# Another order for a fused decay-attention and mixture-of-attention kernel

## The chip, the cores and the metric

The kernel runs on one core of a Trainium2 chip. The metric is the device time of one execution in microseconds (us). Three executions of the kernel before took 305.31, 306.22 and 306.68 us; their median is 306.22 us.

## The reference

Inputs are r, k and v of shape (4 batches, 8 heads, 768 positions, 48 values), a decay w and a bonus u for each head and value, and the weights of four attention experts. The first part is a linear attention with decay; the second takes its output as x (768 rows of 384 for each batch).

```python
for t in range(S):
    kt, vt, rt = (k[:, :, t], v[:, :, t], r[:, :, t])
    cur = np.einsum('bhd,bhe->bhde', u[None] * kt, vt)
    y[:, :, t] = np.einsum('bhd,bhde->bhe', rt, state + cur)
    state = w[None, :, :, None] * state + np.einsum('bhd,bhe->bhde', kt, vt)
...
logits = x @ w_gate            # top 2 of 4 experts, softmax over the two
for e in range(E):
    q, k, v = x @ wq[e], x @ wk[e], x @ wv[e]
    scores = scale * (q @ k.transpose(0, 2, 1))     # causal
    a = softmax(scores)
    out += gate[e] * (a @ v @ wo[e])
```

## The kernel before, in words

The 768 positions of a batch are cut into six chunks of 128, 24 in all; three chunks make a group, of which there are eight. Work is written as small steps, each a Python generator; a step is named with its arguments, as a_quarters,1 (chunk 1) or m_scores,7,1,2 (group 7, expert pair 1, chunk 2 of the group).

The first part, for chunk n: load_chunk loads k and r by DMA from SP's queue (L285, L287), load_vh the values (L292), load_vs a second copy with the halves swapped, for the first six chunks by two copies on ACT (L306). a_decay multiplies k and r by tables of powers of w (DVE for early chunks, else POOL). a_transpose turns k and r on PE (L513) and ACT copies them into kt, rt and rx (L519, L532, L536). a_quarters multiplies them on PE, first k with r (L552), then k with the values (L560). DVE masks the first (a_mask) and sums the second into the running state z (a_sum). a_out multiplies both with values and state (L585, L589), a_add adds the bonus term on DVE, and a_xt turns the result on PE (L620) and copies it on ACT. a_ku and a_own make the bonus term on POOL and DVE.

The second part, for group G: m_values (L686) and m_proj (L661) make values, queries and keys on PE; each product is three matmuls of rounded and rest parts. m_gate ranks the experts on DVE. m_scores makes scores on PE (L738), masks them on DVE (L743) and takes their exponential on ACT (L748). m_weigh scales them on POOL (L761). m_turn turns them on PE (L770), with a copy on ACT (L773). m_av multiplies them with the values (L791) and splits the result into yh (ACT, L798) and yl (DVE, L800). m_out is the last product (L814 to L816), copied on ACT and written by a DMA on SP.

warm_up (six bf16 matmuls of 512 columns, L319) and keep (four transposes, L360) are PE work whose result nobody uses.

What sets the order is the string ORDER: each word is one piece of a step, up to the step's next yield, and the pieces are written in this order, so each engine executes its own in this order. The hex digits behind a slash are the numbers of the buffers or PSUM banks that the piece takes from the rotating ones (the pools have fixed sizes, as eight banks). There is no planner and no scheduler behind it: a wait on an engine holds all that stands behind it there.

## Time and profile before

| | |
|---|---|
| Median of three runs | 306.22 us |
| Span of the profiled execution | 304.7 us |
| PE busy | 292.3 us, 96% |
| DVE, ACT, POOL busy | 206.0, 213.6, 173.2 us |
| DMA moved | 24.83 MB, mean 81 GB/s |

The span is the time from the first to the last instruction of one profiled execution; the page gives no other time for that execution, and the median of the runs stands 1.5 us above it. Busy times of the engines overlap; an engine's idle time matters only where it delays the one that the others wait for. [...] A row of the timeline gives start, duration, engine, line, operation, operands, count, and in brackets the idle time before it and what ended it.

### The profile page before, as it was taken

The numbers are of one execution on the slowest core, as the hardware profiler recorded it, in microseconds if no ns is written. First come the engines' busy times: TensorE is split into PE (matmuls) and PEld (weight loads), VectorE is DVE, ScalarE is ACT, GpSimd is POOL, SyncE is SP. The second block draws the span as 40 slices with busy tenths as digits, with TensorE's granted clock in tenths as the row PEclk, the third lists the DMA queues.
The fourth block names the chain that finished last, engine by engine and source line by source line (L and its number), as shares of the span: only waits on it lengthen the run. The fifth ranks groups of instructions, "written<-read, shape, count | busy, mean of one in ns | idle before, by whom it ended". The sixth has DMA issues, their size and how long they took to land.

```text
span 304.7 us, 13045 instructions
## 1 busy us (share of the span) xinstructions
PE 292.3 (96%) x5518; PEld 248.8 (82%) x5518; DVE 206.0 (68%) x676; ACT 213.6 (70%) x509; POOL 173.2 (57%) x227
## 2 busy tenths in 40 slices
PE   6879999999999999999999999999999999999996
PEld 3669989887898787888789787899799777997775
DVE  7867888889946478477686559468867277675510
ACT  2844687897596694946758794768869775669961
POOL 2969547872995923874454694956292624216420
PEclk9965999999999999999999999999999999999999
DMA  8986324661527327405440436564101200001012
GB/s 157 219 188 118 80 55 107 120 122 25 108 56 166 72 41 159 105 17 105 93 106 1 80 69 141 111 123 102 41 3 41 54 2 31 0 25 56 23 60 77
DMA packets 103310, 24.83 MB, mean 81 GB/s; under 512 B 99794, under 2 KB 103252, under 8 KB 103252
## 3 DMA queue, kind: packets, MB, share of 16 engines
q1 hardware_dynamic: 102688, 23.90, 36.6%
q8 instruction: 43, 0.70, 1.0%
q10 hardware_dynamic: 564, 0.10, 0.2%
q14 instruction: 15, 0.12, 0.1%
HBM read 19.28 MB, written 4.72 MB: 79 GB/s over the span
## 4 chain that ended last, share of the span: by engine, by line
PE 80%; DVE 6%; ACT 5%; issue 2%; POOL 1%; ACTq 0%; DVEq 0%; POOLq 0%
PE banks L661 16%; PE banks L791 11%; PE banks L738 10%; PE banks L686 9%; PE banks L770 8%; PE banks L589 4%; PE banks L552 4%; PE banks L585 4%; PE banks L814 4%; PE banks L513 3%; PE banks L816 3%; PE banks L815 3%; PE banks L560 2%; PE banks L620 2%; ACT rx L536 1%
## 5 line engine op out<-in xcount | busy, mean ns | idle before, releaser
L761 POOL TENSOR_SCALAR pr<-pr,f,gate 128x128 f32<-128x128 f32 (+5 forms) x96 | 67.7, 719 | 72.2 <-DVE f L755 48.7
L743 DVE CUSTOM_DVE_ANT_0 pr<-banks,after 128x256 f32<-128x256 f32 (+5 forms) x96 | 56.5, 620 | 26.7 <-PE banks L738 18.8
L748 ACT ACTIVATE pr<-pr,nm 128x512 f32<-128x512 f32 (+5 forms) x96 | 63.4, 663 | 8.1 <-DVE nm L743 7.7
L773 ACT ACTIVATE pt<-banks 128x768 f32<-128x768 f32 (+1 forms) x64 | 45.6, 731 | 14.8 <-PE banks L770 14.1
L738 PE MATMUL banks<-tk,tq 64*128 64x384 f32 (+3 forms) x384 | 41.5, 338 | 0.2
L791 PE MATMUL banks<-pt,vv 128*64 128x384 f32 (+2 forms) x324 | 40.7, 393 | 0.7 <-DVE yl L800 0.7
L791 PEld LDWEIGHTS banks<-pt,vv 128*64 128x64 f32 x324 | 20.6, 136 | 16.6 <-issue 12.3
L661 PE MATMUL banks<-xt_hi,wqk_hi 128*128 128x384 f32 x96 | 33.5, 349 | 0.6 <-DVE nm L743 0.6
L738 PEld LDWEIGHTS banks<-tk,tq 64*128 64x128 f32 x384 | 30.7, 186 | 3.5 <-issue 1.4
L770 PE MATMUL banks<-ident,pr 64*128 64x64 f32 x672 | 31.6, 227 | 0.9 <-DVE xt_lo L631 0.5
L661 PE MATMUL banks<-xt_hi,wqk_lo 128*128 128x384 f32 x96 | 32.3, 337 | 0.0
L661 PE MATMUL banks<-xt_lo,wqk_hi 128*128 128x384 f32 x96 | 32.3, 336 | 0.0
L770 PEld LDWEIGHTS banks<-ident,pr 64*128 64x128 f32 x672 | 26.2, 139 | 7.1 <-issue 4.2
L612 POOL TENSOR_TENSOR z<-z,w 128x192 f32<-128x192 f32 x20 | 10.1, 506 | 30.4 <-DVE z L608 19.4
L483 POOL TENSOR_TENSOR ku<-kdbuf,uw 128x384 f32<-128x384 f32 x24 | 25.0, 1045 | 2.6 <-DVE banks L492 1.9
L476 POOL TENSOR_TENSOR rdbuf<-rdbuf,tab_r 128x384 f32<-128x384 f32 x22 | 22.7, 1038 | 5.7 <-DMA rdbuf<-in_r_dram 5.7
L585 PE MATMUL banks<-vhbuf,sm 64*64 64x48 f32 x384 | 25.7, 226 | 0.1
L485 POOL TENSOR_TENSOR ku<-ku,rdbuf 128x384 f32<-128x384 f32 x24 | 24.9, 1039 | 1.3
L585 PE MATMUL banks<-vsbuf,sm 64*64 64x48 f32 x384 | 25.2, 226 | 0.0
L686 PE MATMUL banks<-wv_hi,xt_hi 128*128 128x260 f32 x72 | 22.4, 312 | 0.1
L585 PEld LDWEIGHTS banks<-vhbuf,sm 64*64 64x64 f32 x384 | 21.5, 141 | 0.3 <-issue 0.3
L476 POOL TENSOR_TENSOR kdbuf<-kdbuf,tab_k 128x384 f32<-128x384 f32 x21 | 21.5, 1027 | 0.0
(125 smaller groups left out, 723.9 us busy)
## 6 DMA issues: line engine op xcount, KB each, us to landing
kdbuf<-in_k_dram SPq DMA_DIRECT2D x24, 192.0 KB, 3.3
rdbuf<-in_r_dram SPq DMA_DIRECT2D x24, 192.0 KB, 3.6
vhbuf<-in_v_dram SPq DMA_DIRECT2D x24, 192.0 KB, 3.7
out_dram<-o SPq DMA_DIRECT2D x23, 192.0 KB, 1.9
vsbuf<-in_v_dram SPq DMA_DIRECT2D x36, 96.0 KB, 3.2
pr<-in_moe_wv_dram SPq DMA_DIRECT2D x1, 384.0 KB, 4.7
pr<-in_moe_wq_dram SPq DMA_DIRECT2D x1, 384.0 KB, 5.3
pr<-in_moe_wk_dram SPq DMA_DIRECT2D x1, 384.0 KB, 5.4
```

Of the source, the lines that this page charges most:

```text
L476: nc.gpsimd.tensor_tensor(t[:, :, :D], t[:, :, :D], (tab_k, tab_r)[which], op=OP.mult)
L483: nc.gpsimd.tensor_tensor(ku, kd[:, :, :D], uw, op=OP.mult)
L585: nc.tensor.matmul(o, st["sm", n][par][rows, p // 2, i], values, start=fresh, stop=True)
L661: nc.tensor.matmul(ps, a[:, t, m0:m0 + P], x[:, t, :], start=i == 0, stop=i == n - 1)
L686: nc.tensor.matmul(ps, x[:, t, cols], a[:, t, :], start=m == 0, stop=m == n - 1)
L738: nc.tensor.matmul(ps[par][:, n0:n1], tq[rows, part, q], tk[rows, key, n0:n1], start=i == 0, stop=i == 2)
L743: nc.vector.tensor_tensor_reduce(pr_[:, :N], ps[par], after[:, S - N:], 1.0, 3e38, op0=OP.add, op1=OP.min, accum_out=nm)
L748: nc.scalar.activation(pr_[:, :N], pr_[:, :N], AF.Exp, bias=nm, scale=-1.0, accum_out=sums[:, e, j, 0:1])
L761: nc.gpsimd.tensor_scalar(p[:, :N], p[:, :N], f[:, i], gate[:, i, e:e + 1], op0=OP.mult, op1=OP.mult)
L770: nc.tensor.transpose(both[:, x, half], mg[G]["p", e, j][rows, i * C:(i + 1) * C], ident[rows, rows])
L773: nc.scalar.activation(pt.rearrange("s (x half c) -> s x half c", x=n, half=2), both, AF.Copy)
L791: nc.tensor.matmul(psy[par * HD:par * HD + HD, j0 * C:j1 * C], vv[:, i % GC, e, :], mg[G]["t", e, i][:, (j0 - max(0, i - g * GC)) * C:(j1 ...
```

## The change

The string ORDER is replaced: the pieces of all steps stand in another order, and most of them take other buffers and banks of the same pools. The sizes of the pools, the steps and the instructions within a step stay. The table has three lines more, so a line number of the new kernel is three higher than the same line's number before. Its first lines, before and after:

```diff
-warm_up/2 make_ones make_ident load_chunk,0 load_w/0 load_w make_before clear pad,4 pad,0 load_uw powers table,0/0
-powers load_chunk,0 keep,2/2 warm_up/7 warm_up warm_up warm_up load_vh,0 warm_up warm_up table,0 table,1/1 table,1
+make_ident load_w/0 load_chunk,0 warm_up/6 make_ones clear pad,4 warm_up/7 warm_up pad,0 load_w a_transpose,0/4
+load_chunk,0 load_v/7 make_lower powers load_uw table,0/2 table,0 table,1/0 table,1 a_transpose,0/0 a_transpose,0/3
+a_transpose,0/0 make_before table,0/0 load_chunk,1 a_decay,0,0 hi_v load_chunk,1 load_vh,0 powers load_vh,2 table,1
...
```

On PE at the start, from the first a_quarters on, the order before is a_quarters,0 (L552, L560), a_transpose,1 (L513) and a_out,0 (L589 and on). In the rows kdbuf_135 to kdbuf_138 and rdbuf_139 to rdbuf_142 hold k and r, vhbuf_143 to vhbuf_146 the values, of chunks 0 to 3 in turn:

```order
L552 MATMUL banks<-rt_91,kt_89 64x64 x16
L560 MATMUL banks<-vhbuf_143,kdbuf_135 48x48 x16
L513 MATMUL banks<-ident,kdbuf_136 128x64 x8
L513 MATMUL banks<-ident,rdbuf_140 128x64 x8
L589 MATMUL banks<-z_102,rt_91 64x48 x2
L585 MATMUL banks<-vhbuf_143,sm_97 64x48
```

After, from behind a_transpose,1 on (L319 has become L322, the warm-up; L552 L555, L560 L563, L513 L516, L589 L592):

```order
L322 LDWEIGHTS pr_70
L322 MATMUL banks<-pr_70 128x512
L322 LDWEIGHTS pr_70
L322 MATMUL banks<-pr_70 128x512
L555 MATMUL banks<-rt_92,kt_89 64x64 x16
L563 MATMUL banks<-vhbuf_144,kdbuf_136 48x48 x16
L516 MATMUL banks<-ident,kdbuf_137 128x64 x8
L516 MATMUL banks<-ident,rdbuf_141 128x64 x8
L592 MATMUL banks<-z_103,rt_91 64x48 x2
L588 MATMUL banks<-vhbuf_143,sm_97 64x48
```

Four of the six warm-up matmuls have moved behind a_transpose,1, and a_quarters,1 and a_transpose,2 now stand ahead of a_out,0.

On SP's queue of loads at the start, before, from the third DMA to the weights of the values (pr6):

```order
L292 DMA vhbuf0_143<-in_v_dram 128x8x48
L285 DMA kdbuf1_136<-in_k_dram 128x8x48
L287 DMA rdbuf1_140<-in_r_dram 128x8x48
L285 DMA kdbuf2_137<-in_k_dram 128x8x48
L287 DMA rdbuf2_141<-in_r_dram 128x8x48
L292 DMA vhbuf1_144<-in_v_dram 128x8x48
L292 DMA vhbuf2_145<-in_v_dram 128x8x48
L285 DMA kdbuf3_138<-in_k_dram 128x8x48
L287 DMA rdbuf3_142<-in_r_dram 128x8x48
L443 DMA pr6_70<-in_moe_wv_dram 128x12x64
```

After, from the third DMA to the values of chunk 1 (vhbuf1):

```order
L446 DMA pr7_71<-in_moe_wv_dram 128x12x64
L447 DMA wg_166<-in_moe_w_gate_dram 128x3x4
L288 DMA kdbuf1_136<-in_k_dram 128x8x48
L290 DMA rdbuf1_140<-in_r_dram 128x8x48
L295 DMA vhbuf0_143<-in_v_dram 128x8x48
L295 DMA vhbuf2_145<-in_v_dram 128x8x48
L288 DMA kdbuf3_138<-in_k_dram 128x8x48
L290 DMA rdbuf3_142<-in_r_dram 128x8x48
L288 DMA kdbuf2_137<-in_k_dram 128x8x48
L290 DMA rdbuf2_141<-in_r_dram 128x8x48
L295 DMA vhbuf1_144<-in_v_dram 128x8x48
```

The weights have moved from twelfth to third place, and the values of chunk 1 from eighth to thirteenth, behind those of chunk 2 and behind k and r of chunks 3 and 2.

On PE near the end, before, from the last transposes (m_turn,7,3,2, L770) over m_out,6,2 (L814 to L816) to the first matmuls of the last m_av (L791):

```order
L770 MATMUL banks<-ident,pr_70 128x64 x2
L770 MATMUL banks<-ident,pr_66 128x64 x4
L814 MATMUL banks<-wo_hi,yh_82 128x384
L815 MATMUL banks<-wo_lo,yh_82 128x384
L816 MATMUL banks<-wo_hi,yl_83 128x384
L814 MATMUL banks<-wo_hi,yh_81 128x384
L815 MATMUL banks<-wo_lo,yh_81 128x384
L816 MATMUL banks<-wo_hi,yl_84 128x384
L791 MATMUL banks<-pt_75,vv_109 64x128
L791 MATMUL banks<-pt_79,vv_109 64x128
L791 MATMUL banks<-pt_75,vv_109 64x128
L791 MATMUL banks<-pt_79,vv_109 64x128
```

After, from the first part of the last m_av (L794, was L791) to the two m_turn steps behind it (L773, was L770):

```order
L794 MATMUL banks<-pt_79,vv_109 64x128
L794 MATMUL banks<-pt_75,vv_109 64x128
L794 MATMUL banks<-pt_79,vv_109 64x128
L794 MATMUL banks<-pt_75,vv_109 64x128
L794 MATMUL banks<-pt_78,vv_109 64x128
L794 MATMUL banks<-pt_76,vv_109 64x128
L794 MATMUL banks<-pt_78,vv_110 64x128
L794 MATMUL banks<-pt_76,vv_110 64x128
L773 MATMUL banks<-ident,pr_70 128x64 x2
L773 MATMUL banks<-ident,pr_68 128x64 x4
L773 MATMUL banks<-ident,pr_67 128x64 x2
L773 MATMUL banks<-ident,pr_64 128x64 x4
```

The m_out has left this place, the first part of the last m_av has moved ahead of two m_turn steps, and these now stand between its first and its second part.

## Rows read from the trace of the kernel before

**Rows 1.** The page: span, busy share of engines, granted clock, instruction queue.

```profile
span 304.7 us, 13045 instructions
...
PE 292.3 (96%) x5518; PEld 248.8 (82%) x5518; DVE 206.0 (68%) x676; ACT 213.6 (70%) x509; POOL 173.2 (57%) x227
...
PEclk9965999999999999999999999999999999999999
...
q8 instruction: 43, 0.70, 1.0%
```

**Rows 2.** Stretches: length, busy us of PE, PEld, DVE, ACT, POOL, clock, DMA share, GB/s.

```profile
7.00:16.00 9.00, 6.72 (x208) 5.46 (x206) 6.81 (x16) 7.39 (x19) 8.20 (x13) 1.00 1.07 212
...
17.00:18.00 1.00, 1.00 (x52) 1.00 (x52) 0.92 (x3) 0.96 (x3) 0.14 (x1) 0.50 1.18 258
...
22.00:26.00 4.00, 3.51 (x87) 3.23 (x88) 2.78 (x5) 2.05 (x5) 3.92 (x5) 0.50 0.86 166
...
50.00:150.00 100.00, 98.59 (x2051) 84.74 (x2049) 72.36 (x242) 73.38 (x177) 64.50 (x82) 1.00 0.46 96
150.00:290.00 140.00, 139.43 (x2359) 117.29 (x2357) 91.96 (x314) 104.33 (x248) 75.11 (x95) 1.00 0.25 58
```

**Rows 3.** Timeline of PE, first 31 us: start us, duration us, line, count, idle before.

```profile
3.90 2.77 PE L319 MATMUL banks<-pr 128*128 128x512 bf16 x6
...
9.71 0.69 PE L552 MATMUL banks<-rt,kt 48*64 48x64 f32 x32
...
10.70 0.46 PE L513 MATMUL banks<-ident,kdbuf 64*128 64x64 f32 x8
...
11.79 0.26 PE L589 MATMUL banks<-z,rt 48*64 48x48 f32 x2 [0.38 <-ACT z L604]
...
12.86 0.46 PE L513 MATMUL banks<-ident,kdbuf 64*128 64x64 f32 x8
...
14.10 0.36 PE L560 MATMUL banks<-vhbuf,kdbuf 64*48 64x48 f32 x16
16.18 0.40 PE L560 MATMUL banks<-vhbuf,kdbuf 64*48 64x48 f32 x16 [1.72 <-issue]
...
22.36 0.58 PE L620 MATMUL banks<-ident,ownv 64*128 64x64 f32 x6 [0.74 <-DVE ownv L596]
22.73 0.64 PE L513 MATMUL banks<-ident,kdbuf 64*128 64x64 f32 x8
...
23.73 0.46 PE L589 MATMUL banks<-z,rt 48*64 48x48 f32 x8
...
25.82 0.58 PE L686 MATMUL banks<-wv_hi,xt_hi 128*128 128x260 f32 x1
...
28.06 1.13 PE L552 MATMUL banks<-rt,kt 48*64 48x64 f32 x32
...
29.77 0.58 PE L620 MATMUL banks<-ident,ownv 64*128 64x64 f32 x6
...
30.95 0.39 PE L686 MATMUL banks<-wv_hi,xt_hi 128*128 128x260 f32 x1
```

**Rows 4.** SP's own timeline: the issue of vhbuf1 and its neighbour.

```profile
6.34 1.77 SPq L292 DMA_DIRECT2D vhbuf<-in_v_dram  x2
```

**Rows 5.** The page on such loads: count, KB each, median us to landing.

```profile
vhbuf<-in_v_dram SPq DMA_DIRECT2D x24, 192.0 KB, 3.7
```

**Rows 6.** Groups by form: count, busy us and mean ns, idle before.

```profile
L773 ACT ACTIVATE pt<-banks 128x768 f32<-128x768 f32 x48 | 38.4, 811 | 9.6 <-PE banks L770 9.0 <-PE banks L791 0.5
...
L798 ACT ACTIVATE yh<-banks 128x384 fp32r<-128x384 f32 x15 | 7.3, 485 | 5.9 <-PE banks L791 5.9
...
L306 ACT ACTIVATE vsbuf<-vhbuf 64x192 f32<-64x192 f32 x12 | 4.4, 363 | 0.2
```

**Rows 7.** Timeline of PE near the end: first and second part of the last m_av.

```profile
293.45 1.09 PE L791 MATMUL banks<-pt,vv 128*64 128x128 f32 x16
295.25 1.31 PE L791 MATMUL banks<-pt,vv 128*64 128x128 f32 x20 [0.70 <-DVE yl L800]
```

## The prediction

> **What bounds the kernel now.** I read the page first: the span is 304.7 us and PE (TensorE) is busy for 292.3 of it, 96%; DVE, ACT and POOL stay at 57 to 70% [rows 1]. So the matrix engine is the bound, and a new order can only matter where PE waits or where its clock is low. The clock row is all nines but for the third and fourth digit, 15.2 to 30.5 us [rows 1]. [...] What is to be won is therefore in the first 31 us; behind it lie 2.0 us of visible idle time in 240 (1.41 + 0.57).

> In the timeline of PE one sees what went before the drop. [...] At full clock come a_quarters,0 (9.71 to 10.70), a_transpose,1, a_out,0 (11.79 to 12.86). Then, in the middle of a_quarters,1, between two matmuls of the same line, PE stands still for 1.72 us until 16.18 "<-issue": it waited for nothing that another engine did [rows 3]. PE's instructions come by DMA queue q8: 43 packets for 5518 matmuls and 5518 weight loads, 257 instructions each [rows 1]; and the DMA engines are full in this stretch (share 1.07) [rows 2]. I read the wait as a late packet of instructions. In the stretch from 17 us the clock is at half; PE then waits again (0.74 us before 22.36), is without a listed wait from 25.82, and by the digits the clock is back at about 30.5 us.

> The price of the half clock comes from equal steps at both levels [rows 3]: a_out 1.07 us at full (chunk 0, which has 48 of the usual 64 matmuls) and 2.09 at half (chunk 2, 23.73 to 25.82); a_transpose 0.71 (10.70 to 11.79 less its 0.38 wait) and 1.00 (22.73 to 23.73); a_quarters 0.99 and 1.71 (28.06 to 29.77); m_values 2.24 at half (25.82 to 28.06), so some 1.2 at full; a_xt 0.37 at half (22.36 to 22.73) and 0.2 at full.

> **The change, part by part.** No instruction is added on PE but their order is new throughout; the tables of numbers choose other buffers and banks. I split the sum in the start, the middle and the tail.

> *The start, to the point where before stands at 30.95 us.* Four things move. keep (four transposes) leaves the start and goes to the middle, where it costs some 0.2 us of PE. Of the six warm-up matmuls four now stand behind a_transpose,1. On SP the weights wv (384 KB) and chunks 2 and 3 stand ahead of vhbuf1, the values of chunk 1. And a_quarters,1 and a_transpose,2 stand ahead of a_out,0 on PE.

> vhbuf1 was issued at 6.34 with its neighbour [rows 4], and such a load takes 3.7 us to land [rows 5]: about 10 us. It was the eighth tile and is now the thirteenth, wv counted as two. A tile of 192 KB (196,608 bytes) at 212 GB/s [rows 2] takes 0.93 us, so five tiles cost 4.6 us: about 14.6 us. a_quarters,1 needs it on PE, and the ACT copy into vsbuf1 (load_vs) too; ACT works its queue in order, and behind that copy stand tab_k and the copy that a_out,0 wants. Four copies at 0.36 [rows 6] and tab_k at much the same make 16.3 us for the start of a_out,0, where before it started at 11.79. The matmuls of a_quarters,1 and a_transpose,2 are done by then. So a wait for data stands where the wait for instructions stood. The new order has issued as many PE instructions as before had at that wait only inside a_out,0, at about 17 us, which is later than the packet came before (16.18). I take the packet's wait as gone, with 0 to 1.7 us as its bounds.

> [...]

> From 16.3 us I add up in the new order, at half clock: a_out,0 1.6 (48 of 64 of 2.09), a_transpose,3 1.0, a_xt,0 0.4, a_quarters,2 1.7, a_out,1 2.1: 23.1 us. No step of these waits for the step just ahead of it: chunk 3's transposes stand between a_out,0 and a_xt,0, and a_quarters,3 between a_out,1 and a_out,2, so the 0.74 us that a_xt,1 waited has cover. Before, the clock came back some 5 us after PE's last wait (25.82); a run of work without a wait begins at 16.3 to 17.6 us here. I therefore take the clock as back at about 22.4. Then a_out,1 ends 22.8, and at full clock come a_quarters,3 1.0, a_out,2 1.1 (the 1.07 row), a_xt,1 0.2, m_values,0,0 1.2, a_out,3 1.1, a_transpose,4 0.7: 28.1 us. Before has the same done at 30.95 but for a_out,3 (1.1 still owed) and with a_xt,2 (0.2) done in addition: the new order is ahead by 30.95 - 28.1 + 1.1 - 0.2 = 3.7, less keep 0.2: **-3.5 us**. The bounds: at half clock until 30.7 the same sum ends at about 31.7, which makes 0; at full clock from 16.3 on it ends at about 26.0 and makes -5.7; each us of half clock beyond 30.7 costs another 0.5.

> *The middle.* The PE work is the same and DVE, ACT and POOL have room; what can change are short waits. The nearest to one that I find are three: m_av,3,1,0,3 now follows m_turn,3,3,1 directly, whose bank ACT must copy first (0.81 [rows 6]; two thirds of the m_av's own matmuls come ahead of it): 0.2. m_out,2,1 stands one step behind m_av,2,1,0,3, whose copy takes 0.49 on ACT [rows 6] before DVE can subtract: 0.3. a_quarters,5 stands close behind a_transpose,5: 0.2. Of before's 2.0 us idle [rows 2] some will go and others come; I take these as even. Sum **+0.7**, bounds -2.0 (all idle gone) and +3 (as much again as there is, and the three at full price).

> *The tail.* Before, PE waits 0.70 us for DVE's yl ahead of the second part of m_av,7,1 [rows 7]. Two m_turn steps now stand there and cover it. They were taken from the place ahead of the first part, which now follows m_turn,7,3,1 at once, with ACT copies of 0.81 to wait for: 0.6, two copies less the matmuls that lie beside them. **-0.1**, bounds -0.7 and +0.9.

> The sum: 304.7 - 3.5 + 0.7 - 0.1 = 301.8 us of span. The median of the runs is 306.22, 1.5 above the span of the profiled execution; I keep that 1.5 and predict **303.3 us**.

> **The rivals.** *The start stays as it is.* For it: PE waits for data between 13 and 16.3 us in the new order, as it waited for instructions before, and in the stretch from 22 to 26 us before it was busy for 3.51 of 4 and the clock did not come [rows 2]; small matmuls may not bring it back, and m_values comes at about the same time in both. Against it: the waits behind 17.6 us have cover. It makes 304.7 + 0.7 - 0.1 + 1.5 = 306.8.

> *Slower: the clock comes late.* With only two warm-ups at the start PE stands idle from the first transposes until DVE's tables are ready, so the early steps run at half clock too, and the wait for vhbuf1 breaks the work again; if the clock is back only at 34 us or later, 3.4 us at half cost 1.7, and a late packet at the new place up to 1.7 more: 306.8 + 1.7 + 0.3 to 1.7, some 309. It decides from the point where the clock is still at half beyond 31 us. For it: of early waits there are more (a_quarters,1 behind vhbuf1, a_out,0 behind ACT). Against it: those steps wait for DMA and ACT anyway. [...]

> *The clock is not lost at all.* If the four warm-ups and a_quarters,1 keep PE busy enough through the wait, the start gains 5.7: 301.1. Against it: before lost the clock at a gap of 1.72 us.

> **How the numbers follow.** Forecast 0.45, with a range of its own from 301.5 to 305; start unchanged 0.27; clock late 0.20; clock kept 0.08. A measurement of this kernel can tell about 0.5%, 1.5 us: faster is below 304.7, slower above 307.7. Faster takes nearly all of the first case and the last: 0.48. Same takes most of the second and a little of the first: 0.28. Slower has the clock's case and the upper end of the middle's bounds: 0.24. The range from 300.0 to 309.0 leaves out one in ten on either side.

> **What would show it.** In the changed kernel's profile: a wait of PE for DMA or ACT between 13 and 17 us in place of the one "<-issue"; a granted clock of 1.00 in the stretch from 23 to 31 us; a_out,3 done by 28 us; m_av,3,1,0,3 with a wait for ACT; no 0.70 in the tail. The prediction is wrong if the clock stays at 0.50 to 30 us, or if PE's idle time between 50 and 290 us is over 5 us.

## The result and the profile after

| | before | after |
|---|---|---|
| Median | 304.80 us (20 runs, 302.01 to 307.33) | 307.07 us (20 runs, 304.47 to 309.35) |
| Ratio | | 1.0058, 95% interval 1.0034 to 1.0082 |
| Span of the profiled execution | 304.7 us | 305.3 us |

The change makes the kernel slower by 0.6%, some 1.8 us. The forecast was faster by 1% (303.3 us): the time lies in the range, the direction is wrong. With 20 runs the median of before is 1.4 us below that of the three runs that the prediction had. In the runs of the two kernels that list both, the time is 1.7 to 1.8 us above the span; by that the profiled execution of before (304.7) took some 306.4 us, which is at the slow end of the 20.

The page of after, the lines that answer to [rows 1]:

```profile
span 305.3 us, 13035 instructions
...
PE 290.4 (95%) x5517; PEld 247.2 (81%) x5518; DVE 203.6 (67%) x676; ACT 212.3 (70%) x509; POOL 172.6 (57%) x227
...
PEclk9999999999999999999999999999999999999999
...
q8 instruction: 43, 0.70, 1.0%
```

PE is busy for 1.9 us less than before, and the clock row (PEclk, the granted clock in tenths of the full one) has no low digit any more; still the span is not shorter. The table by stretches, with one stretch, 26 to 30 us, added to those of [rows 2] (length, busy us of PE, PEld, DVE, ACT, POOL, clock, DMA share, GB/s):

```profile
7.00:16.00 9.00, 8.64 (x141) 6.00 (x145) 6.96 (x13) 5.68 (x16) 6.94 (x10) 1.00 1.01 205
17.00:18.00 1.00, 1.00 (x44) 0.89 (x43) 0.90 (x4) 0.97 (x4) 1.00 (x2) 1.00 1.27 256
22.00:26.00 4.00, 2.00 (x128) 1.88 (x127) 2.14 (x7) 1.80 (x4) 2.92 (x5) 1.00 0.78 157
26.00:30.00 4.00, 3.25 (x111) 2.99 (x113) 1.86 (x5) 1.60 (x4) 2.91 (x4) 1.00 0.34 67
...
50.00:150.00 100.00, 98.67 (x2061) 86.31 (x2060) 73.66 (x252) 74.38 (x185) 65.47 (x83) 1.00 0.43 87
150.00:290.00 140.00, 138.86 (x2326) 116.92 (x2328) 90.03 (x311) 102.20 (x243) 72.65 (x93) 1.00 0.25 57
```

From 17 us on the clock is 1.00, as forecast, but between 22 and 30 us PE is busy for only 5.25 of 8 us. The 1.00 of the first row, and the nines ahead of it in the clock row, say less: the first clock record of this trace is the rise at 15.7 us, the views print full clock ahead of it, and a_quarters,0 there takes 1.71 us (10.47 to 12.18 below), which was its length at half clock. PE's timeline shows with what (compare [rows 3]; line numbers are three higher):

```profile
2.92 1.01 PE L322 MATMUL banks<-pr 128*128 128x512 bf16 x2 [2.92 <-DVE banks L355]
...
10.47 1.13 PE L555 MATMUL banks<-rt,kt 48*64 48x64 f32 x32
...
12.18 0.69 PE L516 MATMUL banks<-ident,kdbuf 64*128 64x64 f32 x8
...
13.63 1.49 PE L322 MATMUL banks<-pr 128*128 128x512 bf16 x3 [0.33 <-issue]
15.05 0.98 PE L555 MATMUL banks<-rt,kt 48*64 48x64 f32 x32
...
16.31 0.46 PE L516 MATMUL banks<-ident,kdbuf 64*128 64x64 f32 x8
...
16.95 0.55 PE L592 MATMUL banks<-z,rt 48*64 48x48 f32 x3
...
22.34 0.20 PE L588 MATMUL banks<-vhbuf,sm 64*64 64x48 f32 x1 [1.19 <-issue]
...
26.75 0.25 PE L588 MATMUL banks<-vhbuf,sm 64*64 64x48 f32 x1 [2.42 <-issue]
...
29.07 0.33 PE L592 MATMUL banks<-z,rt 48*64 48x48 f32 x8
...
30.18 0.46 PE L516 MATMUL banks<-ident,kdbuf 64*128 64x64 f32 x8
...
33.51 0.34 PE L664 MATMUL banks<-xt_hi,wqk_hi 128*128 128x384 f32 x1
```

At 22.34 and at 26.75, inside a_out,1 and a_out,2, PE stands still for 1.19 and 2.42 us for nothing that another engine did. It is the wait of 1.72 us that before had once. The last row is the first m_proj, which I use as a mark of the start's end: it begins at 33.51 us here, with a_out,3 (29.07 to 30.18) already done, and at 33.21 in before's trace:

```profile
33.21 0.34 PE L661 MATMUL banks<-xt_hi,wqk_hi 128*128 128x384 f32 x1
```

In that execution the clock stayed up behind the waits; its time, 307.01 us, is still the middle of after's 20. A second profile of after, the same stretch by windows, and PE's wait in it (here and below a line can stand one to four lines further down than in after or before):

```profile
22.00:26.00 4.00, 1.93 (x128) 1.80 (x127) 2.28 (x7) 1.95 (x4) 3.34 (x5) 1.00 0.65 128
26.00:30.00 4.00, 3.93 (x49) 3.55 (x49) 1.11 (x2) 1.22 (x3) 2.48 (x3) 0.50 0.51 103
30.00:33.00 3.00, 3.00 (x87) 2.85 (x86) 2.02 (x5) 0.38 (x1) 0.00 (x0) 0.53 1.08 238
```

```profile
26.07 0.34 PE L589 MATMUL banks<-vhbuf,sm 64*64 64x48 f32 x1 [2.14 <-issue]
```

The wait is there again (2.14 us), and the clock falls behind it: 0.50 from 26 to 30 us. Here the first m_proj begins at 35.40 us.

What the traces of the runs show up to 40 us: when the clock was at half (us; a first rise ahead of 9 us is left out), PE's waits with no releaser (less 0.3 us ahead of the moved warm-ups), and the first m_proj. The ratio is to runs of before made beside it and leaves disturbed runs out. The median of before itself went from 304.8 to 306.1 us between these sets, so rows compare by their ratios and not by their medians. What each run is, the next section tells.

| run | median us, ratio, interval | half clock | "<-issue" waits | first m_proj |
|---|---|---|---|---|
| before | 304.80 | 17.0 to 30.7 | 1.72 | 33.21 |
| before, second profile (b_again) | 305.55 (1 run) | 17.7 to 27.9 | 2.04 | 32.18 |
| after | 307.07, 1.0058, 1.0034 to 1.0082 | to 15.7 | 1.19, 2.42 | 33.51 |
| after, second profile (a_again) | 307.73 (1 run) | to 15.8, 26.0 to 32.8 | 0.64, 2.14 | 35.40 |
| bw | 305.88, 0.9993, 0.9961 to 1.0024 | 9.6 to 16.4, 23.3 to 30.1 | none | 33.66 |
| bsp | 307.57, 1.0052, 1.0028 to 1.0075 | 15.1 to 32.2 | none | 35.24 |
| c1 | 306.17, 1.0056, 1.0019 to 1.0093 | 12.4 to 19.2, 26.1 to 29.5 | 0.4, 2.1 | 33.87 |
| d2 | 304.31, 1.0014, 0.9974 to 1.0054 | to 15.9, 26.2 to 29.6 | 0.27, 1.59 | 33.11 |
| e1 | 307.23, 1.0018, 0.9983 to 1.0052 | to 16.7 | 0.53 | 32.19 |
| a_fill | 305.91, 1.0012, 0.9983 to 1.0042 | to 14.1 | none over 0.3 | 32.84 |
| c2 | 305.38, 1.0026, 0.9992 to 1.0059 | 16.5 to 19.9 | 0.3, 1.9 | 31.45 |
| c2_fill | 306.55, 1.0037, 1.0005 to 1.0069 | 14.0 to 20.8 | 0.5 | 33.49 |
| s2_fill | 305.77, 1.0002, 0.9972 to 1.0032 | 14.3 to 21.2 | 0.5, 0.5 | 32.93 |
| b_fill | 303.76, 0.9967, 0.9933 to 1.0001 | none | none | 29.97 |
| b_best | 305.22, 1.0012, 0.9976 to 1.0047 | none | 0.5 | 30.28 |
| b_fill6 | 304.06, 0.9957, 0.9928 to 0.9985 | none | 0.7 | 30.45 |
| h1 | 312.39, 1.0249, 1.0185 to 1.0312 | 18.0 to 28.2, 35.1 to 38.5 | 0.3 | 34.70 |
| h2 | 308.63, 1.0153, 1.0104 to 1.0202 | 9.5 to 16.3, 26.6 to 30.0 | 2.1 | 34.57 |
| m1 | 309.79, 1.0106, 1.0055 to 1.0157 | to 14.4, 28.0 to 31.4 | 1.1, 2.1 | 34.57 |

Two rows of after that answer to [rows 4] and [rows 7], the issue of vhbuf1 on SP, and the two parts of the last m_av on PE:

```profile
11.12 0.87 SPq L295 DMA_DIRECT2D vhbuf<-in_v_dram  x1
```

```profile
293.70 1.35 PE L794 MATMUL banks<-pt,vv 128*64 128x128 f32 x14 [0.17 <-ACT pt L776]
...
295.74 1.31 PE L794 MATMUL banks<-pt,vv 128*64 128x128 f32 x20 [0.18 <-DVE yl L803]
```

vhbuf1 is issued at 11.12 where it was 6.34, and the 0.70 us in the tail have become 0.17 and 0.18.

### The profile page after: what moved, and what is told of

Its sections match the earlier page's. It is cut to its first block, busy times and chain, and to the rows that moved or that the text cites. A ratio compares the mean times of both kernels' runs of the same rounds, so it can differ in the third digit from the quotient of the medians.

```text
span 305.3 us, 13035 instructions
## 1 busy us (share of the span) xinstructions
PE 290.4 (95%) x5517; PEld 247.2 (81%) x5518; DVE 203.6 (67%) x676; ACT 212.3 (70%) x509; POOL 172.6 (57%) x227
## 4 chain that ended last, share of the span: by engine, by line
PE 83%; ACT 5%; issue 3%; DVE 3%; DMA 3%; POOL 2%; SPq 0%; ACTq 0%; DVEq 0%
PE banks L664 15%; PE banks L794 12%; PE banks L741 10%; PE banks L773 8%; PE banks L689 8%; PE banks L516 4%; PE banks L555 4%; PE banks L817 4%; PE banks L592 4%; PE banks L588 4%; PE banks L819 3%; PE banks L818 3%; PE banks L563 3%; PE banks L623 2%; POOL pr L764 2%
## 5 line engine op out<-in xcount | busy, mean ns | idle before, releaser
L764 POOL TENSOR_SCALAR pr<-pr,f,gate 128x128 f32<-128x128 f32 (+5 forms) x96 | 68.2, 726 | 58.1 <-DVE f L758 30.2
L746 DVE CUSTOM_DVE_ANT_0 pr<-banks,after 128x256 f32<-128x256 f32 (+5 forms) x96 | 56.7, 621 | 23.5 <-PE banks L741 17.7
L751 ACT ACTIVATE pr<-pr,nm 128x256 f32<-128x256 f32 (+5 forms) x96 | 63.3, 663 | 10.9 <-DVE nm L746 10.8
L776 ACT ACTIVATE pt<-banks 128x768 f32<-128x768 f32 (+1 forms) x64 | 45.2, 730 | 16.8 <-PE banks L773 14.3
L794 PE MATMUL banks<-pt,vv 128*64 128x384 f32 (+2 forms) x324 | 41.0, 393 | 0.4 <-DVE yl L803 0.2
L794 PEld LDWEIGHTS banks<-pt,vv 128*64 128x64 f32 x324 | 20.8, 136 | 16.6 <-issue 12.2
L773 PEld LDWEIGHTS banks<-ident,pr 64*128 64x128 f32 x672 | 26.0, 139 | 8.2 <-issue 2.5
L773 PE MATMUL banks<-ident,pr 64*128 64x64 f32 x672 | 31.5, 228 | 0.9 <-POOL pr L764 0.9
L588 PE MATMUL banks<-vhbuf,sm 64*64 64x48 f32 x384 | 24.6, 219 | 3.6 <-issue 3.6
L615 POOL TENSOR_TENSOR z<-z,w 128x192 f32<-128x192 f32 x20 | 10.2, 509 | 27.3 <-DVE z L611 25.9
L588 PE MATMUL banks<-vsbuf,sm 64*64 64x48 f32 x384 | 24.3, 220 | 0.9 <-DMA vsbuf<-in_v_dram 0.9
L588 PEld LDWEIGHTS banks<-vhbuf,sm 64*64 64x64 f32 x384 | 20.4, 134 | 3.9 <-issue 3.9
```

Source lines behind the costliest of these rows:

```text
L588: nc.tensor.matmul(o, st["sm", n][par][rows, p // 2, i], values, start=fresh, stop=True)
L746: nc.vector.tensor_tensor_reduce(pr_[:, :N], ps[par], after[:, S - N:], 1.0, 3e38, op0=OP.add, op1=OP.min, accum_out=nm)
L751: nc.scalar.activation(pr_[:, :N], pr_[:, :N], AF.Exp, bias=nm, scale=-1.0, accum_out=sums[:, e, j, 0:1])
L764: nc.gpsimd.tensor_scalar(p[:, :N], p[:, :N], f[:, i], gate[:, i, e:e + 1], op0=OP.mult, op1=OP.mult)
L773: nc.tensor.transpose(both[:, x, half], mg[G]["p", e, j][rows, i * C:(i + 1) * C], ident[rows, rows])
L776: nc.scalar.activation(pt.rearrange("s (x half c) -> s x half c", x=n, half=2), both, AF.Copy)
```

## The experiments

**Which part: joining the two orders.** h1 has before's order up to its first m_proj and then after's, h2 the reverse; words already done are left out, and buffers are numbered anew where they clash.

```diff
 before: h1, from the joint on
-m_proj,0,1,0/5 a_transpose,4/02 a_mask,3/03 m_proj,0,1,0/1
+make_sums,1 load_o,1/5 load_vh,4 load_vh,5 a_mask,3/23
...
 after: h2, from the joint on
-m_proj,0,0,0/6 m_proj,0,0,1/7 a_transpose,4/0 a_own,3/0
+keep,2/7 a_decay,5,0 a_own,3/1 a_decay,5,1 a_ku,5/0
...
```

> The order of before up to its first m_proj, and behind it the order of after with what was already done left out. Theory F (instruction blocks): after's start keeps the clock at full from 15.7 us on, but PE's instructions come in blocks of 256 that take some 4.4 us from one boundary to the next while the loads run, so the start gains only 0.3 to 0.8 us; the loss lies behind the start. So this one should be at least as slow as after: span about 305.5 to 306.5, time 307 to 308. Rival S (the start itself loses, the rest is even): like before, 304.5 to 305.5.

> The order of after up to its first m_proj, and behind it the order of before. F: 304.0 to 304.8, level with before or up to 0.8 us faster. Rival S: like after, 306.5 to 307.5. In the trace both expect waits of PE of 1 to 2.5 us with no releaser inside a_out,1 and a_out,2.

Measured: 312.39 (1.0249, 1.0185 to 1.0312) and 308.63 us (1.0153, 1.0104 to 1.0202), both slower than either kernel. At the joint stand waits that neither has: in h1 1.5 us for DVE's z at 33.2 and 1.4 us for xt_lo at 44.2, with the clock at half from 35.1 to 38.5; in h2 1.5 us for ownv at 40.9. So both expectations missed, and the joint says nothing about the parts. I read the parts from unbroken traces instead: from the first m_proj to the end, before takes 271.54 and 271.65 us in its two profiles, after 271.78 and 270.62.

**The early edits.** c1 puts after's warm-ups back to the start; bw moves them in before; bsp gives before the loads of after.

```diff
 after: c1
-make_ident load_w/0 load_chunk,0 warm_up/6 make_ones clear pad,4 warm_up/7 warm_up pad,0 load_w a_transpose,0/4
+make_ident load_w/0 load_chunk,0 warm_up/6 make_ones clear pad,4 warm_up/7 warm_up warm_up warm_up warm_up warm_up pad,0
...
 before: bw
-a_transpose,1/1 load_chunk,2
+a_transpose,1/1 warm_up warm_up warm_up warm_up load_chunk,2
 before: bsp, behind the second load_chunk,0
+load_v/6 load_chunk,1 load_chunk,1 load_vh,0 load_vh,2 load_chunk,3 load_chunk,3 load_chunk,2 load_chunk,2 load_vh,1
```

> After, with the four warm-up matmuls put back to the start. F: the early steps run at full clock (about 2 us sooner), the clock falls at the waits between 13 and 18 us, and PE then needs some 4 us for 256 instructions at half clock, which is what a block takes anyway: 306 to 307.5, no more than 1 us from after. Rival C (the clock held through the start is worth its full 3 us): 309 to 310.

> Before, with the last four warm-up matmuls put behind a_transpose,1 as in after. If the clock then comes up at 14 to 16 us as in after's profiles: the steps from 6 to 13 us run at half clock, the second block boundary is crossed at 17 to 18 us in place of 16.2 to 16.7, and behind it the clock stays up longer than in before: first m_proj at 32 to 34 us, time 305 to 307. Rival (the early half clock lies beside waits for DMA and DVE and costs nothing): second boundary at 16.2 to 16.7, time 303.5 to 305.

> Before, with the first loads on SP in the order of after (weights of the values third, chunk 3 ahead of chunk 2, values of chunk 1 thirteenth); PE, ACT, DVE and POOL keep before's order. PE meets a_transpose,2 and a_quarters,1 with their data 2 to 4 us late, so the second block boundary is crossed at 18 us or later: 307 to 309. Rival (the boundary is set by the block alone, the data are in time): 305 to 306.

c1 is level with after (1.0056), and bw with before (0.9993, with the clock at half until 16.4 and the boundary crossed at 17.7 as its theory says, but no loss): where the four warm-ups stand costs nothing on the whole that these runs can tell. c1 crosses the second boundary at 18.0, behind waits of 1.4 us for ACT's rt and 1.5 us for vhbuf1. bsp alone is as slow as after (1.0052). Its trace has the price; PE's longest wait, then the stretch from 16 to 30 us:

```profile
16.51 0.69 PE L517 MATMUL banks<-ident,kdbuf 64*128 64x64 f32 x7 [2.82 <-DVE rdbuf L478]
```

```profile
16.00:30.00 14.00, 12.52 (x307) 11.49 (x308) 10.72 (x26) 7.79 (x17) 10.27 (x12) 0.50 0.85 174
```

a_transpose,2 waits 2.82 us for chunk 2, which is now behind the weights and chunk 3. The second boundary is crossed at 18.7 us, in before at 16.18, and the clock, which fell at 15.1, stays at half until 32.2.

**What the wait is.** d2 leaves out the loads of k, r and v of chunks 4 to 7; e1 moves long matmuls into the wait; a_fill puts matmuls there that nobody reads.

```diff
 d2
-nc.sync.dma_start(kt[:, :, :D], k[b, :, s, :].rearrange("h s d -> s h d"))
+if n not in range(4, 8): nc.sync.dma_start(kt[:, :, :D], k[b, :, s, :].rearrange("h s d -> s h d"))
...
 e1
-a_out,2 a_ku,2 a_own,2/0 a_decay,4,0 load_chunk,5 make_lower a_xt,1/1 a_xt,1 m_values,0,0/0 m_values,0,0/1
+m_values,0,0/0 a_out,2 a_ku,2 a_own,2/0 a_decay,4,0 load_chunk,5 make_lower a_xt,1/1 a_xt,1 m_values,0,0/1
 a_fill
+    def fill(i):
+        ps = take("ps")[:, :H * D]
+        nc.tensor.matmul(ps, ident, tab_r.rearrange("p h d -> p (h d)"), start=True, stop=True)
...
-a_out,1 a_add,1 a_transpose,3/00 a_quarters,3/43
+fill,0/4 a_out,1 a_add,1 a_transpose,3/00 a_quarters,3/43
-a_out,2 a_ku,2
+fill,1/2 fill,2/7 a_out,2 a_ku,2
```

> After, with the loads of k, r and v of chunks 4 to 7 left out (their buffers keep the contents of chunks 0 to 3, so the results are others). F: with the DMA engines free from about 16 us on, the blocks arrive sooner, and the waits with no releaser (1.19, 2.42 and 0.7 us in after) shrink to 1 us in all: 303.5 to 304.5. Rival L (a block takes its 4.4 us whatever the loads do): the waits stay, 306.5 to 307.5.

> After, with m_values,0,0 (9 long matmuls) moved on PE from behind a_xt,1 to between a_quarters,3 and a_out,2, that is ahead of the block boundary at which after waits 2.42 us. Theory F (a block of 256 instructions can't come sooner than some 4.2 us after the boundary before it): 1.2 us of work now lie in the wait, which shrinks to about 1.2 us, and the clock falls less often behind it: 1 to 2.5 us faster than after, 304.5 to 306. Rival D (the wait is for something else that PE needs, the data of a_out,2): the wait keeps its length behind m_values, and the time stays at 307 +-0.5.

> After, with three idle-time matmuls added on PE (identity by tab_r, 128x384 in f32, into a free bank, nobody reads them): one ahead of a_out,1 and two ahead of a_out,2, that is ahead of the two block boundaries where PE waits 0.6 to 1.2 and 2.1 to 2.4 us. Theory F with V (the waits are for instruction blocks and end at the same moment whatever PE does meanwhile; the clock falls behind them in most executions, for 3.4 to 6.8 us, at 0.5 us per us): the waits shrink by the length of the added work, the blocks come when they came, the clock stays up: 305.0 to 306, 1 to 2 us faster than after. Rival (added work is paid in full, the clock is not decided there): 308.5 to 309.5.

In d2 the DMA engines are almost idle when the block is waited for, and PE still waits 1.59 us. Two stretches, and the wait:

```profile
20.00:22.00 2.00, 1.73 (x121) 1.60 (x117) 1.61 (x6) 1.95 (x5) 1.10 (x2) 1.00 0.04 8
22.00:26.00 4.00, 2.41 (x151) 2.23 (x145) 2.33 (x7) 1.88 (x4) 3.60 (x5) 1.00 0.01 4
```

```profile
25.19 0.25 PE L588 MATMUL banks<-vhbuf,sm 64*64 64x48 f32 x1 [1.59 <-issue]
```

From one boundary to the next a block takes 3.6 to 3.7 us there (17.9 to 21.6, 21.6 to 25.19), with all loads 3.5 to 4.6 where I can read it (22.34 to 26.75 in after), and 5.5 to 6.0 for the first block of before. Most of it is there without the loads as well: in the waits the rival L was nearer than F as I had put it, while the time, 304.31 us, is F's. What d2 gains in time (1.0014 against 1.0058, intervals that overlap) I have not separated.

In e1 the wait shrinks to 0.53 with m_values ahead of it, but the next stands behind it, for a copy of values on ACT. PE's two rows:

```profile
25.36 0.26 PE L592 MATMUL banks<-z,rx 48*64 48x48 f32 x2 [0.53 <-issue]
...
27.95 0.26 PE L588 MATMUL banks<-vsbuf,sm 64*64 64x48 f32 x2 [0.99 <-ACT vsbuf L309]
```

The profiled span is 303.4 us, with the clock up all the way; of the 12 times four lie from 304.02 to 305.15 and eight from 306.12 to 308.23; in all eight the clock fell for a time, in the four only once (by the lists of clocks below). So the waits are for blocks, as F says, but a shorter wait is no sure gain: the median (307.23) is that of the rival D, and the interval of the ratio (1.0018) and after's overlap.

In a_fill the block comes about when it would have come (the boundaries are crossed at 22.3 and 25.7 us), and the waits at both boundaries are gone. The stretch from 16 to 30 us:

```profile
16.00:30.00 14.00, 13.24 (x470) 10.75 (x470) 10.69 (x29) 8.96 (x21) 10.32 (x13) 1.00 0.84 171
```

The added work is not paid (ratio 1.0012 against 1.0058): the rival is out. What a_fill holds is the clock, and by the ratios that is worth 0.46%, 1.4 us, of after's loss (the intervals overlap, so the size is not sure).

**Two profiles more**, of the unchanged kernels:

> Before, unchanged, for a second profile of its start. Theory V (the clock's fall and return in the first 35 us differ from execution to execution, and 302 to 308 us in the times of before is that): other times of fall and return than 17.0 and 30.7 us, and the first m_proj at another time than 33.2 us, by 1 us or more. Rival: the same to 0.3 us.

> After, unchanged, for a second profile. V: the wait of 2.4 us in a_out,2 is there again, and behind it the clock falls to half for some us, which it did not in the first profile: the first m_proj at 34 to 35 us in place of 33.5. Rival: the clock stays at full from 15.7 us on, and the first m_proj is at 33.5.

Both as V says (after's mark, 35.40, a little later still); their numbers stand in the table. In the profiles with after's own start and its wait of 2.1 to 2.4 us (after, a_again, h2, m1) the clock fell behind the wait three times in four.

The lists of all executions bear V out: beside each time stands the mean granted clock. Of the 129 executions of before that the ratios of the experiments rest on, 8 have a clock of 1.00 and took 302.1 to 303.0 us; 31 have some 0.988 and took 303.7 to 306.4; 49 have some 0.983 and took 304.6 to 306.8; 41 have 0.978 or less and took 305.8 to 308.2. That is 0.3 us for each us at half clock (a straight line through the 129). Of after's executions that count, 5 of 18 have 1.00, and these took 304.8 to 307.0 us, some 3 us more than before at that clock; the mean clock of the 18 is 0.994, of the 129 it is 0.984. So behind its first rise after keeps the clock better than before and is slower all the same. The lists leave out what lies ahead of the first clock record, though, and that is at 15.7 us in after's trace and at 6.8 in before's. They also show that the sets differ: beside c1, d2, h1 and h2 the mean clock of before was 0.988, and at 0.983 c1 took 306.4 us on the mean and before 305.6, less of a difference than c1's ratio has.

**Waits behind the start.** m1 moves load_vs,13 and m_scores,7,1,0 forward, with the banks behind numbered anew.

```diff
-m_scores,7,1,2/14 m_turn,7,0,2/6 m_turn,7,0,1/4 m_turn,7,0,2/5 m_scores,7,1,0/01 m_turn,7,0,1/0
+m_scores,7,1,2/14 m_scores,7,1,0/45 m_turn,7,0,2/6 m_turn,7,0,1/0 m_turn,7,0,2/5 m_turn,7,0,1/0
-load_chunk,14 m_turn,1,3,0/2 a_xt,9/0 a_xl,9/0 a_out,10 m_turn,1,3,2/0 load_vs,13 m_turn,1,3,1/4
+load_chunk,14 m_turn,1,3,0/2 a_xt,9/0 a_xl,9/0 a_out,10 m_turn,1,3,2/0 load_vs,13 load_vs,13 m_turn,1,3,1/4
...
```

> After, with its two longest new waits behind the start taken away: the second DMA of load_vs,13 is issued earlier on SP (0.9 us wait of a_out,13), and m_scores,7,1,0 goes ahead of m_turn,7,0,2 on PE (0.7 us wait for POOL). If each wait is on the path: 1.3 to 1.6 us faster than after, 305.4 to 305.8, and then the loss behind the start is these two. Rival: another wait follows in the same place and half or less is won: 306.3 to 307.

Measured 309.79 us (1.0106, 1.0055 to 1.0157): no gain on after, rather a loss (the intervals overlap); both missed. PE's row, and the stretches around it:

```profile
283.80 1.80 PE L741 MATMUL banks<-tk,tq 64*128 64x384 f32 x11 [1.62 <-ACT pt L776]
```

```profile
276.00:284.00 8.00, 6.24 (x75) 4.50 (x73) 6.24 (x23) 6.17 (x15) 5.18 (x6) 1.00 0.00 1
284.00:287.40 3.40, 3.40 (x17) 3.08 (x15) 0.83 (x2) 2.28 (x6) 0.00 (x0) 0.50 0.02 5
287.40:300.00 12.60, 11.26 (x144) 7.71 (x142) 2.26 (x8) 8.31 (x17) 5.19 (x6) 1.00 0.09 32
```

The moved m_scores took the wait for POOL away and made one of 1.62 us for a bank that ACT copies; behind it the clock fell for 3.4 us, late in the kernel. The wait for vsbuf (0.91 us in after's profile) comes in one of after's two profiles only: a_again doesn't have it.

**Taking both back.** c2 puts the warm-ups and vhbuf1 back in after (and ACT's load_vs,2 behind a_xt,0); c2_fill adds the three matmuls of a_fill; s2_fill also loads chunk 2 ahead of chunk 3.

```diff
 after: c2
-load_vh,0 powers load_vh,2 table,1
+load_vh,0 powers load_vh,1 table,1
...
 s2_fill
-a_decay,1,0 load_chunk,3 load_chunk,3
+a_decay,1,0 load_chunk,2 load_chunk,2
```

> After, with the six warm-up matmuls at the start as in before, the values of chunk 1 (vhbuf1) loaded ahead of those of chunk 2 on SP, and ACT's two copies of load_vs,2 put behind a_xt,0's copy. If the late vhbuf1 and the early half clock are what sets back the first block boundaries (the second crossed at 17.9 us, in before at 16.2): it is crossed at 16 to 16.7, and the two blocks behind it follow 1 to 2 us sooner, with waits of 2 us each and a fall of the clock behind them: first m_proj at 32.5 to 33.5, time 305 to 306.5. Rival (another wait of the early steps, for ACT's or POOL's queue, takes the place of vhbuf1's): second boundary at 17.5 or later, time 306 to 307.5.

> The same with the three matmuls of the run before last but one (a_fill) ahead of a_out,1 and a_out,2. If early steps and waits for blocks are all of the loss of after's start: clock at full from 6 us on, first m_proj at 31 to 32 us, time 303 to 304.5, level with before with its own added matmuls (303.76). Rival as above: 305 to 306, like a_fill.

> After, with six warm-ups at the start, the values of chunk 1 ahead of those of chunk 2, chunk 2 ahead of chunk 3 on SP (as in before), and the three added matmuls of a_fill. If the early steps and the waits for blocks are the whole of after's loss: second boundary at 16 to 16.7 us, clock at full to the end, first m_proj at 31 to 32 us, time 303 to 304.5. Rival (PE's order with a_quarters,1 and a_transpose,2 ahead of a_out,0 waits early whatever the loads do): 305.5 to 306.5, as c2_fill.

c2 came out as its theory says (second boundary at 16.5, 305.38 us; the first m_proj, 31.45, even sooner, but that profile is of the fastest of its 12 executions). c2_fill (306.55 us) missed both its theory and its rival: DVE waited longer for chunk 2 in it, a_transpose,2 stood 1.6 us, and the boundary was crossed at 18.3. s2_fill crosses at 16.4 and is level with before (1.0002, an interval just clear of after's), without reaching the 304.5 of its theory; its time is the rival's, and a_quarters,1, now ahead of a_out,0, waits 1.4 to 1.5 us for ACT's rt in all three.

**A faster version.** The same matmuls in before: b_fill has two ahead of a_quarters,1 and two ahead of a_out,1; b_fill6 two more, ahead of a_xt,1 and m_values,0,0; b_best is b_fill with a_xt,1 behind a_transpose,3 and m_values,0,0 in bank 7 (and other banks for four steps behind it).

```diff
 before: b_fill6
-load_vh,1 a_quarters,1/27
+load_vh,1 fill,0/7 fill,1/0 a_quarters,1/27
-a_out,1 a_add,1 a_xt,1/0
+fill,2/6 fill,3/3 a_out,1 a_add,1 fill,4/6 a_xt,1/0
-a_xt,1 m_values,0,0/3
+a_xt,1 fill,5/6 m_values,0,0/3
```

> Before, with four such matmuls added: two ahead of a_quarters,1 and two ahead of a_out,1, where the first two blocks are waited for. If the half clock from 17 to 28 or 31 us is what keeps before's start long, and the blocks alone hold PE at full clock: first m_proj at 30 to 31 us in place of 32.2 to 33.2, time 302.5 to 304, faster than both. If the block after next is late as well at full clock (256 instructions in 2 us), the clock falls there instead: 304.5 to 306, no gain. Rival (added work is paid in full): 307 to 308.

> Before with the four added matmuls of b_fill, and two changes of order: a_xt,1 behind the transposes of chunk 3 on PE, and m_values,0,0 in a bank (7) that nobody reads any more. If the two waits of 0.94 us of b_fill are on the path: first m_proj at 28.5 to 29.5 us, 302 to 303.5. Rival (the next instruction block takes their place): like b_fill, 303.5 to 304.5.

> Before with the four added matmuls of b_fill and two more, ahead of a_xt,1 and of m_values,0,0, where b_fill waits 0.94 us each. If the clock falls at these waits in some executions of b_fill: fewer times above 305 us than b_fill's 4 of 12, median 303.2 to 303.8. Rival: paid in full, 304 to 305.

b_fill6 is faster than before beyond the interval (0.9957, 0.9928 to 0.9985, 304.06 us), with 2 of 12 times above 305 us (b_fill 4); its median lies in the range of the rival (304 to 305), not at the 303.2 to 303.8 that was expected. b_fill (303.76 us) is where its theory has it; its interval just touches 1. In b_fill6's trace, from 16 to 30 us and from the first m_proj:

```profile
16.00:30.00 14.00, 13.25 (x382) 10.54 (x374) 11.93 (x24) 8.11 (x18) 12.35 (x13) 1.00 0.86 175
```

```profile
20.68 0.27 PE L593 MATMUL banks<-z,rt 48*64 48x48 f32 x3 [0.66 <-issue]
...
30.45 0.34 PE L665 MATMUL banks<-xt_hi,wqk_hi 128*128 128x384 f32 x1
```

The clock is up where it was at half in before, and the first m_proj begins 1.7 to 2.8 us sooner. In the lists all 12 executions of b_fill6 have a clock of 1.00 and took 303.2 to 305.9 us, where before at that clock took 302.1 to 303.0: the added matmuls cost more than 1 us, and win because before has that clock in only 8 of 129 executions. b_best missed both its theory and its rival: it still waits 0.7 us for ownv, has new waits of 1.2 us for nm (DVE, at 52) and 0.7 us for xt_lo, and gains nothing.

## Why the prediction was wrong

**The step that failed** is the sum of the start, "-3.5 us", and in it two sentences. "I take the packet's wait as gone": it came back at the next two boundaries, 0.6 to 1.2 and 2.1 to 2.4 us; the sum looked at the one boundary alone, where PE in fact waits no more. And "at full clock come a_quarters,3 1.0, a_out,2 1.1": the walk adds up durations of steps, as if their instructions were there. From the start of a_out,0 to the end of a_transpose,4 it has 11.8 us (16.3 to 28.1); the first profile of after took 14.0 (16.95 to 30.99), although the clock was up all the way, which the walk had only from 22.4, and 3.6 of it are the two waits. The rows at hand could have told. A usual a_quarters and a_out are 128 matmuls and 128 weight loads, one block of 256; by [rows 3] they last 2.1 us at full clock and 3.8 at half, while the first block of before, entered at 10.7, let PE wait for the next until 16.18. Where a block takes 3.5 us or more, PE waits in such a stretch at full clock (1.19 and 2.42 us in after), and half clock costs less than the sum has for it (0.3 us for each us by the times of before, not 0.5). My bounds for the start (-5.7 to 0) did not hold this, since "0" was the half clock kept and not a full clock with waits. One reading in it is wrong as well: the last wait listed in [rows 3] ends at 22.36 and not at "PE's last wait (25.82)", so the "some 5 us" behind the clock's return at 22.4 stand on no row; that the clock was up still sooner, from 15.7, is luck.

**What the start really does.** First m_proj: 33.21 and 32.18 in before, 33.51 and 35.40 in after, less 1.1 for a_out,3, makes after later by 0.7 on the mean. keep costs 0.53 in the middle, from its first matmul to the next step's (0.2 in the forecast). For the rest, 271.6 in before and 271.2 in after, with a_out,3 and keep reckoned, leave +0.2, where the middle and the tail stood at +0.7 and -0.1. Together +1.4, of 1.8 measured (interval 1.0 to 2.5); with two profiles each, that is as close as it gets.

**What causes it.** Shown: at full clock PE waits for blocks of instructions in the start, 3.6 us in one profile of after and 2.8 in the other; these waits shrink when long matmuls are put ahead of them (0.53 us in e1), go when matmuls that nobody reads fill them (none over 0.3 in a_fill), and for the most part stay when the loads beside them are left out (1.9 us in d2). The sum had nothing for them. Shown as well: after's order of loads costs before 0.52% by itself (bsp). That this is what after loses (0.58%) is not shown, though the numbers are alike: bsp loses by a wait of 2.82 us for chunk 2 and a clock at half until 32.2, and after has neither. The late load was in the sum ("So a wait for data stands where the wait for instructions stood"), where the two waits were taken for one. It does set the second boundary back (17.9 against 16.2 us), but so do the moved warm-ups: the boundary comes at 17.7 with these alone (bw), at 18.0 without them (c1), and at 16.5 when both are taken back (c2). And a late boundary is not yet a loss, as bw shows.

Not settled: how the loss is shared among the loads, PE's own order and the later first rise of the clock, since c2 (1.0026), s2_fill (1.0002) and a_fill (1.0012) have intervals that overlap with each other's, and those of c2 and a_fill with after's.

**The other steps.** vhbuf1 is issued 4.8 us later (4.6 in the forecast). a_out,0 starts at 16.95 (16.3 in the forecast), but without a wait of PE for data, since the warm-ups and early steps at half clock fill the time to 15.05; that the two starts are so near is luck. The clock is at 1.00 from 23 to 31 us in one profile and not in the other. a_out,3 is done at 30.2, not 28. m_av,3,1,0,3 has no listed wait for ACT, m_out,2,1 neither. The tail's 0.70 us went, as forecast. Of the two signs by which the prediction was to be wrong neither came in the first profile (the clock at half to 30 us; over 5 us idle from 50 to 290, where it is 2.5): they did not test the step that failed.

**The rivals.** "The start stays as it is" (306.8) was nearest in time to 307.07, for another reason than its own. "The clock comes late" had the mechanism in part, "a late packet at the new place": that deserved the higher chance. In the two traces the clock was not late (15.8 us at the latest); it was lost a second time in one of them, and by the lists in 13 of 18 executions, though for less time than in before.

## What to carry to other kernels

Count instructions as well as microseconds: where PE runs many small matmuls at full clock, it may use up a block of instructions faster than the next one comes (here 256 in 2.1 us, where the next came 3.5 to 4.6 us behind the one before), and a faster clock or a better order then only moves the wait. Put the few long matmuls between the many short ones there (here the wait went from 2.42 to 0.53 us, though the time of that run is not surely better), or at least something that keeps the clock up (in a_fill it is at 1.00 from 16 to 30 us). And a load moved forward moves others back (vhbuf1 by 4.8 us here): price the last of them, not only the first. Before a forecast, look at more than one execution: here the clock of the profiled one was among the lowest of its kernel.

## What was not expected of the hardware

PE's waits of over 0.35 us without a releaser stand at fixed places of its list of records (weight loads, matmuls and semaphore steps), or one record on: behind the 448th in before and b_again, the 704th and 960th in after, a_again, c1 and m1, the 960th in c2, d2, e1, h2 and s2_fill, and the 1728th (0.7 us, up to 44.94 in after): 256 apart or a multiple of it. In before and after the packet on q8 (16 KB) ahead of such a wait starts 1.9 to 3.1 us after PE has crossed the boundary before (13.78 behind 10.70 in before; 19.87 behind 17.92, 24.35 behind 22.34 and 42.33 behind 40.43 in after), takes 0.9 to 1.3 us, and PE goes on 1.2 to 1.6 us behind its end. Up to 31 us each packet among small matmuls starts 0.6 to 3.1 us behind the boundary before it in these two traces; the one among long matmuls starts sooner (in before at 28.06 us, where the 960th record is reached at 28.34).

The time of one execution of before scatters from 302.0 to 307.3 us, and the two profiles show where from: the clock was at half for 13.7 us in one and 10.2 in the other, and the first m_proj stood 1.0 us apart. The listed clocks of the other executions (above) show the same.
